# A linear-attention block and an MLP mixer in one kernel: y and the state products get PSUM banks of their own, and the masks change places

## The chip, the cores and the metric

The kernel runs on one core of one Trainium2 chip. A core has a matrix engine (TensorE, PE in the profile), three engines for elementwise work (VectorE, DVE; ScalarE, ACT; GpSimd, POOL) and a queue that issues transfers (SyncE, SP). Matrix products land in PSUM, which has eight banks of 512 fp32 values per partition; DVE and ACT take them out of it. The metric is the device time of one execution in microseconds (us). The kernel before takes 544.54 us, the median of three runs (543.99 to 545.38).

## The reference

The input is four sequences of 768 tokens with 8 heads of 48 channels. The first block is a recurrence with a state of 48 x 48 per head, the second an MLP mixer that takes its output as `x`, 384 channels per token. All is fp32.

```python
for t in range(S):
    cur = einsum('bhd,bhe->bhde', u * k[t], v[t])
    y[t] = einsum('bhd,bhde->bhe', r[t], state + cur)
    state = w[t][:, None] * state + einsum('bhd,bhe->bhde', k[t], v[t])
# mixer, on x = y with the heads side by side
xt = x.transpose(0, 2, 1)
u = x + (relu(xt @ w_tok1) @ w_tok2).transpose(0, 2, 1)
out = u + relu(u @ w_ch1) @ w_ch2
```

## The kernel before, in words

**Units.** The recurrence is cut into chunks of 64 tokens. A unit is 256 tokens of one sequence (two blocks of 128, four chunks) with all heads, so a sequence is three units and the whole is twelve (`NU`). Units 0 to 2 belong to the first sequence. For a unit, DVE scans the decays (`ends`, `begins`), multiplies keys and queries by them (`keys`, `queries`), PE makes the products of keys and queries inside each chunk (`gram`, line 248), and DVE writes them to `at` with a mask that keeps the strictly earlier tokens (`mask`, line 406). The token's own product, with `u`, goes to the diagonal of `at`: in units 0 to 3 by a second set of products (`own_gram`) that is picked out of PSUM with a predicated copy (`own_put`, line 260); in units 4 to 11 by sums that DVE makes from rows of r, k and `u_rows` (`products`, `sums_put`, lines 383 to 393).

**State.** `tokens` turns the keys with PE (line 278) and ACT copies them out (`copied`, line 279). `carry` (`outer`, line 295) makes the state products `kv`, one bank for each parity of chunk. Then four pairs follow each other: ACT scales the state (`scaled`, line 419), DVE adds `kv` to it (`updates`, lines 427 and 429).

**Output.** `across` (line 308) multiplies the scaled states by the queries into `y` in PSUM. A tiny ACT copy from `y` (`seen`, line 314) stands behind it. `within` (line 322) adds `at` times v to the same `y`, and ACT copies `y` to `x` in three pieces (`taken`, line 328).

**PSUM.** The pool `ps_a` has one tile of two banks under the tag "a", which both `kv` and `y` use; unit 2 alone takes its `kv` from `ps_m`. While units 0 to 2 are issued, `ps_g` holds two grams of two banks and `ps_m` two single banks. After that both are closed and `ps_m` has six single banks for all else: grams, turned keys, and the mixer's results. A tile's bank goes to the next tile once the last instruction that reads the first has ended.

**Mixer.** It works a sequence behind: `hidden` and `back` (lines 497 to 506) mix tokens, `turn` (line 512) transposes, `up` (line 520, with a relu on ACT at line 522) and `quarters` or `down` (lines 591 to 652) mix channels, and a result `o` is stored per 128 tokens. The last sequence uses another form of `up` (`thirds`, line 552).

**Weights.** They come as 64-bit floats in two raw buffers, `scratch` and `spare`, and are converted by DVE and ACT in steps (`convert`, lines 200 to 218; ACT's are lines 203, the power, and 209, the sign). A raw buffer is loaded again once its last reader has ended (line 197).

**Order.** PE, DVE and ACT issue in exactly the order in which `strict` receives the steps (line 88); SP's transfers are placed by the compiler's scheduler. For units 0 to 2 that order is a list written out by hand (lines 700 to 708). For units 3 to 11 each unit has a list of steps with costs (line 676), and `woven` (line 46) merges the lists of three units with the pieces of the mixer by the midpoints of their costs, as shares of each list's total. The range test (`ranges`, line 348) is an ACT step in these lists. The function `by_halves` is a path for inputs outside the range and is not run here.

## Time and profile before

| | |
|---|---|
| median of three runs | 544.54 us |
| the profiled execution, its own time | 542.25 us |
| its span | 540.5 us |
| PE busy, share of the span | 503.2 us, 93% |
| DVE busy | 335.9 us, 62% |
| ACT busy | 212.4 us, 39% |
| mean granted clock of TensorE | 0.981 |
| PE busy from 0 to 57 us (units 0 to 2) | 34.2 us |
| DVE busy from 0 to 57 us | 46.3 us |
| PE busy from 57 to 135 us (units 3 and 4 begin) | 72.8 us |
| PE busy from 290 to 390 us | 99.7 us |

The span is that of one profiled execution, from its first to its last instruction; the execution's own time is 1.75 us more, and the median of the runs without a profile another 2.29 us more. In rows of the timeline the numbers are the start and the length in us, then the engine, the line of the program, the operation, what it writes from what it reads, the shape and how many are merged into the row; in brackets stands how long the engine had been idle before, and what ended that. In rows of the waits the numbers are the total in us, how often, and the longest. One fp32 product stands as two matmul records. In rows of the windows they are start and end, length, PE's busy time and records, the granted clock as a share of full speed, the busy share of the transfer engines and GB/s.

### The profile page before, as it was taken

What the parts mean: (1) busy time and instruction counts of PE and PEld (TensorE: products, weight loads), DVE (VectorE), ACT (ScalarE), POOL (GpSimd) and SP (SyncE); (2) the same over time, 40 slices, a digit from 0 to 9 for tenths busy, and PEclk for the clock granted to TensorE, in tenths of its full rate; (3) what the DMA queues carried; (4) which work ended last, traced back from release to release, by engine and by line L of the source; (5) the groups of instructions that cost most, each with busy time, mean ns of one, the idle gap of its engine ahead of it and who ended that gap; (6) DMA issues with size and microseconds to landing.
All of it is one profiled execution on the core that took longest, in us unless ns stands there. A gap on an engine that the chain in (4) does not pass through costs nothing.

```text
span 540.5 us, 12631 instructions
## 1 busy us (share of the span) xinstructions
PE 503.2 (93%) x5542; PEld 434.2 (80%) x5542; DVE 335.9 (62%) x514; ACT 212.4 (39%) x525; POOL 1.3 (0%) x10
## 2 busy tenths in 40 slices
PE   3468889899799999999899999999999999999997
PEld 3356568677698967898898967898898977999996
DVE  7987899878671755194372656277295525775654
ACT  3857686571134333423324233523514313541400
POOL 0000000000000000000000000000000000000000
PEclk9689999899899999999999999999999999999999
DMA  8867647723212404104113112102000000000000
GB/s 312 330 178 190 232 156 237 185 78 104 84 59 70 119 29 129 46 16 150 37 59 107 52 59 98 31 3 89 2 24 7 2 31 1 1 1 31 1 32 32
DMA packets 20941, 46.01 MB, mean 85 GB/s; under 512 B 2128, under 2 KB 13008, under 8 KB 20880
## 3 DMA queue, kind: packets, MB, share of 16 engines
q1 hardware_dynamic: 20736, 45.14, 26.4%
q8 instruction: 45, 0.74, 0.6%
q14 instruction: 16, 0.13, 0.1%
q10 hardware_dynamic: 144, 0.00, 0.0%
HBM read 40.41 MB, written 4.72 MB: 83 GB/s over the span
## 4 chain that ended last, share of the span: by engine, by line
PE 83%; DVE 11%; ACT 4%; issue 1%; DMA 1%; DVEq 0%; ACTq 0%
PE q_ps L609 27%; PE z_ps L520 24%; PE z_ps L552 6%; PE h_ps L497 5%; PE h_ps L504 5%; PE gram L248 3%; PE h_ps L591 3%; PE y_ps L308 3%; PE y_ps L322 2%; PE kv_ps L295 2%; PE k_ps L278 2%; DVE to_end L356 1%; PE xT_ps L512 1%; DVE w L364 1%; ACT before L419 1%
## 5 line engine op out<-in xcount | busy, mean ns | idle before, releaser
L520 PE MATMUL z_ps<-xT,wch 128*128 128x256 f32 x648 | 148.6, 384 | 1.1 <-DVE wch L218 1.0
L520 PEld LDWEIGHTS z_ps<-xT,wch 128*128 128x128 f32 x648 | 121.1, 191 | 18.2 <-DVE wch L218 1.4
L609 PE MATMUL q_ps<-wch,z 128*128 128x192 f32 x492 | 87.0, 328 | 0.0
L609 PEld LDWEIGHTS q_ps<-wch,z 128*128 128x128 f32 x492 | 80.4, 190 | 1.3 <-DVE z L651 0.3
L522 ACT ACTIVATE z<-z_ps 128x256 f32<-128x256 f32 x108 | 40.9, 382 | 83.0 <-PE z_ps L520 82.2
L609 PE MATMUL q_ps<-scratch,z 128*128 128x192 f32 x324 | 58.1, 333 | 0.0
L419 ACT ACTIVATE before<-state,to_end 112x48 f32<-112x48 f32 x176 | 44.2, 324 | 27.0 <-DVE state L429 25.7
L609 PEld LDWEIGHTS q_ps<-scratch,z 128*128 128x128 f32 x324 | 54.4, 194 | 0.2
L429 DVE TENSOR_TENSOR state<-before,kv_ps 112x192 f32<-112x192 f32 x40 | 13.9, 349 | 42.8 <-ACT before L419 29.7
L504 PE MATMUL h_ps<-h,wtok 128*128 128x384 f32 x96 | 35.4, 493 | 0.6 <-ACT h L499 0.6
L497 PE MATMUL h_ps<-x,wtok 128*128 128x384 f32 x96 | 32.2, 489 | 1.3 <-DVE state L429 1.3
L619 DVE TENSOR_TENSOR o<-x,z 128x192 f32<-128x192 f32 x8 | 2.9, 358 | 47.6 <-ACT z L618 46.7
L506 DVE TENSOR_TENSOR x<-x,h_ps 128x384 f32<-128x384 f32 x24 | 13.3, 552 | 28.2 <-PE h_ps L504 28.1
L356 DVE TENSOR_TENSOR_SCAN to_end<-w,starts 112x1041 f32<-112x1041 f32 (+1 forms) x13 | 28.1, 2160 | 2.1 <-DMA w<-in_w_dram 1.7
L497 PEld LDWEIGHTS h_ps<-x,wtok 128*128 128x128 f32 x96 | 17.9, 190 | 13.2 <-issue 1.6
L364 DVE TENSOR_TENSOR_SCAN w<-w,starts 112x1041 f32<-112x1041 f32 x12 | 27.8, 2320 | 0.0
L348 ACT ACTIVATE junk<-to_end,least 112x1041 uint8<-112x1041 f32 x12 | 13.9, 1161 | 28.3 <-DVE to_end L356 28.3
L328 ACT COPY x<-y_ps 64x384 f32<-64x384 f32 (+1 forms) x36 | 17.1, 474 | 19.6 <-PE y_ps L322 19.3
L308 PE MATMUL y_ps<-before,rk 48*64 48x48 f32 x704 | 14.5, 226 | 11.0 <-DVE state L429 10.9
L504 PEld LDWEIGHTS h_ps<-h,wtok 128*128 128x128 f32 x96 | 16.6, 190 | 10.1 <-ACT h L499 2.8
L308 PEld LDWEIGHTS y_ps<-before,rk 48*64 48x64 f32 x704 | 13.1, 140 | 14.3 <-issue 9.4
L513 ACT COPY xT<-xT_ps 128x384 f32<-128x384 f32 x24 | 11.3, 476 | 22.5 <-PE xT_ps L512 22.4
(136 smaller groups left out, 665.8 us busy)
## 6 DMA issues: line engine op xcount, KB each, us to landing
rk<-in_rk_dram SPq DMA_DIRECT2D x36, 192.0 KB, 3.7
near<-in_near_dram SPq DMA_DIRECT2D x8, 768.0 KB, 4.4
w<-in_w_dram SPq DMA_DIRECT2D x11, 520.5 KB, 3.4
spare<-in_w_ch_dram SPq DMA_DIRECT2D x10, 512.0 KB, 4.5
vt<-in_v_dram SPq DMA_DIRECT2D x12, 384.0 KB, 4.6
out_dram<-o SPq DMA_DIRECT2D x24, 192.0 KB, 1.9
scratch<-in_w_ch_dram SPq DMA_DIRECT2D x8, 512.0 KB, 4.7
rk<-in_rk_dram SPq DMA_DIRECT2D x6, 512.0 KB, 8.5
```

The source lines that it names most:

```text
L248: fours(lambda q, j, rows, cols: pe.matmul(g[q][cols, ts(ca, T)], k_[rows, ds(ca * 128 + j * T, T)], r_[rows, ds(ca * 128 + j * T, T)], st ...
L308: pe.matmul(y[put(q, j), q, ds((c * A + a) * D, D)], r_[q * P:q * P + D, ds((c * A + a) * 128 + j * T, T)], before[g][q * P:q * P + D, a, ...
L328: return [lambda: act.copy(x[:, 0], got[:, 0])] + [lambda n=n: act.copy(x[ts(n, P), 1], got[ts(1 - n, P), 1]) for n in range(2)]
L356: dve.tensor_tensor_scan(to, of, start, 0.0, op0=ALU.mult, op1=ALU.add)
L364: dve.tensor_tensor_scan(w_[:ROWS], w_[:ROWS], starts[:ROWS], 0.0, op0=ALU.mult, op1=ALU.add)
L419: act.mul(t[:ROWS, a], state[bt, g][:ROWS, a], by_last(c, j)[:, a:a + 1])
L497: pe.matmul(sums[i], wtok1[:, c, ts(i, 128)], x_of()[:, c, :], start=(c == 0), stop=(c == C - 1))
L504: pe.matmul(ps, wtok2[:, i, ts(c, 128)], h1[:, i, :], start=(i == 0), stop=(i == DTOK // 128 - 1))
L520: pe.matmul(ps, wch1[:, m, ts(jt, 128)], xT[:, m, ts(s, SEG)], start=(m == 0), stop=(m == DM // 128 - 1))
L522: act.activation(zs[s][:, jt, :], ps, AF.Relu)
L552: pe.matmul(ps[:, q], lefts[r][:, ts(q, 128)], of[r], start=first and q == 0, stop=end and q == JB - 1, skip_group_check=True)
L609: pe.matmul(ps, a[:, j, :], b[:, j, :], start=(j == 0), stop=(j == HJ - 1))
```

## The change

It has four parts.

1. *Banks.* `kv` of all units of the first sequence (0 to 2) is put in the two single banks of `ps_m`; from unit 3 on it stays in `ps_a`. `y` of units 0 and 1 stays in `ps_a`, that of unit 2 goes to a tile of `ps_g`, and from unit 3 on `y` is two single banks of `ps_m`.
2. *Masks.* In units 0 to 3 the diagonal is put first, by a multiplication that writes all of `at` (with an fp32 mask that lies in `u_rows` until that is loaded), and the masked gram second, by a predicated copy. For unit 3 the diagonal's step moves from behind the mask to just behind its products, and the load of `u_rows` from the end of the hand-written list to behind that step.
3. *View.* The tiny copy from `y` is a step of its own, with a place in the lists; with `y` in two tiles it is two copies.
4. *Order.* The hand-written list of units 0 to 2 is rearranged.

```diff
--- before.py
+++ after.py
@@ -123,7 +123,8 @@
     ones = const.tile([128, 1], f32, name="ones")
     ident = const.tile([128, 128], f32, name="ident")
     strictly = const.tile([128, T], f32, name="strictly")
-    diagonal = const.tile([128, T], u8, name="diagonal")
+    on_diagonal = u_rows[:, :T]
+    diagonal, before_it = (const.tile([128, T], u8, name=name) for name in ("diagonal", "before_it"))
 
     def load_w(i):
         if i < NU:
@@ -166,11 +167,13 @@
 
     make_identity(nc, ident)
     for j in range(2):
-        dve.tensor_copy(diagonal[ts(j, T)], ident[ts(j, T), ts(j, T)])
+        dve.tensor_copy(on_diagonal[ts(j, T)], ident[ts(j, T), ts(j, T)])
+    dve.tensor_copy(diagonal, on_diagonal)
     pool.memset(strictly, 1.0)
     for j in range(2):
         pool.affine_select(out=strictly[ts(j, T)], in_=strictly[ts(j, T)], compare_op=ALU.is_gt, fill=0.0, base=0,
                            pattern=[[1, T]], channel_multiplier=-1)
+    dve.tensor_copy(before_it, strictly)
 
     wtok1 = wts.tile([128, C, DTOK], f32, name="wtok1")
     wtok2 = wts.tile([128, DTOK // 128, S], f32, name="wtok2")
@@ -296,36 +299,45 @@
                                   vt[ts(j, T), c, ts(2 * a + q, D)], start=True, stop=True)
         return kv
 
-    def across(r_, before, half):
-
-        y = ps_a.tile([128, 2, 512], f32, name="y_ps", tag="a")
+    def across(r_, before, half, where=None):
+
+        where = where or (ps_g and (ps_a, "a"))
+        both = where and where[0].tile([128, 2, 512], f32, name="y_ps", tag=where[1])
+        y = [both[:, q] for q in range(2)] if where else [bank("y_ps") for q in range(2)]
         begun = set()
         for c in range(UC):
             for a in range(A):
                 for q, j in ((0, 0), (1, 0), (1, 1), (0, 1)):
                     g = 2 * (half * UC + c) + j
                     if g > 0:
-                        pe.matmul(y[put(q, j), q, ds((c * A + a) * D, D)],
+                        pe.matmul(y[q][put(q, j), ds((c * A + a) * D, D)],
                                   r_[q * P:q * P + D, ds((c * A + a) * 128 + j * T, T)],
                                   before[g][q * P:q * P + D, a, :], start=(q, j) not in begun, stop=False,
                                   skip_group_check=True)
                         begun.add((q, j))
-        seen = apool.tile([128, 2], f32, name="seen")
-        act.copy(seen, y[:, :, X * D - 1])
-        return y
+
+        def see():
+            seen = apool.tile([128, 2], f32, name="seen")
+            if where:
+                act.copy(seen, both[:, :, X * D - 1])
+            else:
+                for q in range(2):
+                    act.copy(seen[:, q:q + 1], y[q][:, X * D - 1:X * D])
+
+        return y, see
 
     def within(y, at, vt):
 
         for ca in reversed(range(X)):
             c, a = divmod(ca, A)
             for q, j in ((0, 0), (0, 1), (1, 1), (1, 0)):
-                pe.matmul(y[put(q, j), q, ts(ca, D)], at[ts(j, T), q, ca, :], vt[ts(j, T), c, ts(2 * a + q, D)],
+                pe.matmul(y[q][put(q, j), ts(ca, D)], at[ts(j, T), q, ca, :], vt[ts(j, T), c, ts(2 * a + q, D)],
                           start=False, stop=ca == 0, skip_group_check=True)
 
     def put_in(x, y, half):
         x = x[:, ts(half, UC), :].rearrange("p c (a q e) -> p q c a e", a=A, q=2)
-        got = y[:, :, :X * D].rearrange("p q (c a e) -> p q c a e", c=UC, a=A)
-        return [lambda: act.copy(x[:, 0], got[:, 0])] + [lambda n=n: act.copy(x[ts(n, P), 1], got[ts(1 - n, P), 1]) for n in range(2)]
+        got = [y[q][:, :X * D].rearrange("p (c a e) -> p c a e", c=UC, a=A) for q in range(2)]
+        return [lambda: act.copy(x[:, 0], got[0])] + [lambda n=n: act.copy(x[ts(n, P), 1], got[1][ts(1 - n, P)]) for n in range(2)]
 
     def unit(i):
 
@@ -375,7 +387,8 @@
             L["own"] = grams(L.pop("uk"), r_)
 
         def own_put():
-            pick(at, diagonal, L.pop("own"))
+            for q, g in L.pop("own"):
+                dve.tensor_mul(at[:, q], g, over_heads(on_diagonal, g.shape[1]))
 
         def products(n):
             t = nears[i]
@@ -402,11 +415,13 @@
             L["gram"] = grams(k_, r_)
 
         def mask():
+            if i <= UB:
+                return pick(at, before_it, L.pop("gram"))
             for q, g in L.pop("gram"):
                 dve.tensor_mul(at[:, q], g, over_heads(strictly, g.shape[1]))
 
         def carry():
-            L["kv"] = outer(L.pop("kT"), vs[i], half, apart=i == UB - 1)
+            L["kv"] = outer(L.pop("kT"), vs[i], half, apart=bt == 0)
 
         def by_last(c, j):
             return of_chunks(L["to_end"], 1, 1)[:, :, 0].rearrange("p (x j) -> p x j", j=2)[:, ts(c, A), j]
@@ -431,7 +446,10 @@
         def before():
             if half == 0:
                 xs[bt] = xpool.tile([128, C, DM], f32, name="x")
-            L["y"] = across(r_, L["before"], half)
+            L["y"], L["see"] = across(r_, L["before"], half, (ps_g, "gram") if i == UB - 1 else None)
+
+        def seen():
+            L["see"]()
 
         def after():
             within(L["y"], at, vs[i])
@@ -446,7 +464,7 @@
         return dict(ranges=each(ranges, 2), ends=ends, keys=keys, begins=begins, queries=queries, own_u=each(own_u, A),
                     own_gram=own_gram, copied=each(copied, UC), taken=each(taken, 3),
                     own_put=own_put, products=[lambda n=n: products(n) for n in range(3)], sums_put=sums_put,
-                    tokens=tokens, gram=gram, mask=mask, carry=carry, before=before, after=after,
+                    tokens=tokens, gram=gram, mask=mask, carry=carry, before=before, seen=seen, after=after,
                     scaled=[lambda c=c, j=j: scaled(c, j) for c in range(UC) for j in range(2)],
                     updates=[lambda c=c, j=j: update(c, j) for c in range(UC) for j in range(2)])
 
@@ -675,12 +693,12 @@
         some = lambda fs, c: [(c, f) for f in fs]
         return [(0.1, lambda: (load_rk(i + 2), load_v(i + 1))), *([] if by_tokens else some(e["own_u"], 0.2)),
                 (2.4, e["ends"]), (1.2, e["keys"]), (0.4, e["ranges"][0]), (2.2, e["begins"]), (1.0, e["tokens"]), (0.2, e["copied"][0]),
-                *([] if by_tokens else [(1.0, e["own_gram"])]), (0.2, e["copied"][1]), (1.2, e["queries"]), (0.3, by[0]),
+                *([] if by_tokens else [(1.0, e["own_gram"]), (1.3, e["own_put"]), (0.1, lambda: sp.dma_start(u_rows, u_all))]), (0.2, e["copied"][1]), (1.2, e["queries"]), (0.3, by[0]),
                 (1.0, sums[0]), (1.0, e["carry"]), (1.0, sums[1]),
                 (0.7, up[0]), (0.3, by[1]), (1.4, e["gram"]), (1.0, sums[2]), (0.1, lambda: load_near(i + 1)),
                 (0.7, up[1]), (0.3, by[2]), (1.2, e["mask"]), (0.7, up[2]), (0.3, by[3]),
-                (1.3, e["sums_put"] if by_tokens else e["own_put"]), (0.4, e["ranges"][1]), (0.7, up[3]),
-                (0.1, lambda: load_w(i + 2)), (1.0, e["before"]), (1.0, e["after"]), *some(e["taken"], 0.3),
+                *([(1.3, e["sums_put"])] if by_tokens else []), (0.4, e["ranges"][1]), (0.7, up[3]),
+                (0.1, lambda: load_w(i + 2)), (1.0, e["before"]), (0.1, e["seen"]), (1.0, e["after"]), *some(e["taken"], 0.3),
                 *(some(make_lefts(i - NU + UB), 0.7) if i >= NU - UB else [])]
 
     hiddens, turned, ups, downs = mixing_of(0)
@@ -698,14 +716,14 @@
     s0, s1, s2 = (e["updates"] for e in (e0, e1, e2))
     t0, t1, t2 = (e["scaled"] for e in (e0, e1, e2))
     strict(*e0["own_u"], e0["ends"], e0["own_gram"], e0["begins"], e0["keys"], e0["tokens"], *e0["copied"], e0["queries"], lambda: load_w(2),
-           e0["gram"], *e1["own_u"], e1["ends"], e0["carry"], *e0["ranges"], e0["mask"], e0["own_put"], e1["own_gram"], s0[0], t0[1],
-           x0, p0, s0[1], t0[2], m0, g0, e1["begins"], s0[2], t0[3], add0, s0[3], t1[0], e0["before"], put0, load2,
+           e0["gram"], *e1["own_u"], e1["ends"], e0["carry"], *e0["ranges"], e0["own_put"], e0["mask"], e1["own_gram"], s0[0], t0[1],
+           x0, p0, s0[1], t0[2], m0, g0, e1["begins"], s0[2], t0[3], add0, s0[3], t1[0], e0["before"], e0["seen"], put0, load2,
            e1["keys"], e0["after"], *e2["own_u"], e1["tokens"], *e1["copied"], e1["queries"], e1["carry"], *e0["taken"], lambda: load_v(2),
-           e1["gram"], e2["ends"], e2["keys"], s1[0], t1[1], e2["tokens"], e2["begins"], e2["copied"][0], s1[1], t1[2], e2["copied"][1],
-           e2["carry"], e1["mask"], s1[2], t1[3], e1["own_put"], e2["own_gram"], s1[3], t2[0], e2["queries"], e2["gram"], e1["before"],
-           s2[0], t2[1], x1, p1, m1, e1["after"], s2[1], t2[2], e2["mask"], *h[:4], s2[2], t2[3], e2["own_put"], *e1["taken"], add1, g1,
-           s2[3], e2["before"], put1, to_ch[0][0], e2["after"], *h[4:8], x2, m2, *e2["taken"], p2, add2, g2, *h[8:], put2,
-           lambda: (load_w(3), load_rk(3), load_v(UB), load_w(4), load_rk(4)), to_ch[1][0], lambda: sp.dma_start(u_rows, u_all))
+           e1["gram"], e2["ends"], e2["keys"], s1[0], t1[1], e2["tokens"], e1["own_put"], e2["own_gram"], s1[1], t1[2], *e2["copied"],
+           e2["begins"], e2["carry"], s1[2], t1[3], e1["mask"], s1[3], t2[0], e1["before"], e2["queries"], e2["gram"], s2[0], t2[1], e1["seen"],
+           e1["after"], x1, m1, s2[1], t2[2], e1["taken"][0], *h[:4], e2["own_put"], s2[2], t2[3], e1["taken"][1], p1, e2["mask"], e1["taken"][2],
+           s2[3], e2["before"], e2["seen"], add1, g1, put1, to_ch[0][0], e2["after"], *h[4:8], x2, m2, *e2["taken"], p2, add2, g2, *h[8:], put2,
+           lambda: (load_w(3), load_rk(3), load_v(UB), load_w(4), load_rk(4)), to_ch[1][0])
 
     six_banks.close()
     ps_g, ps_m = None, six_banks.enter_context(tc.tile_pool(name="ps_m", bufs=6, space=bass.MemoryType.PSUM))
@@ -825,7 +843,8 @@
                         else:
                             dve.tensor_mul(new[:ROWS], states[g][:ROWS], by[:, ts(c, A), j].unsqueeze(2).to_broadcast([ROWS, A, D]))
                             dve.tensor_add(new[:ROWS], new[:ROWS], got)
-            y = across(r_, states, half)
+            y, see = across(r_, states, half)
+            see()
             within(y, at, vt)
             for f in put_in(x, y, half):
                 f()
```

## The prediction

> **What bounds the kernel now.** First the page: TensorE (PE) is busy for 503.2 of 540.5 us and carries 83% of the chain that ended last, so a microsecond counts only where PE idles or runs slowly. Its whole idle time is 37 us. The waits of PE name most of it (total us, times, longest):
>
> ```profile
> PE y_ps L308 <- DVE state L429: 10.9, 4, 3.9
> PE gram L248 <- DMA rk<-in_rk_dram: 8.3, 1, 8.3
> PE kv_ps L295 <- ACT x L328: 2.0, 1, 2.0
> ...
> PE y_ps L322 <- ACT seen L314: 1.1, 4, 0.3
> ```
>
> The first row is the change's subject: line 308 (`across`) waits for a state update. The PE timeline finds the four places (start, duration; idle before in brackets):
>
> ```profile
> 23.15 1.94 PE L308 MATMUL y_ps<-before,rk 48*64 48x48 f32 x48 [3.86 <-DVE state L429]
> ...
> 102.51 1.14 PE L308 MATMUL y_ps<-before,rk 48*64 48x48 f32 x48 [2.01 <-DVE state L429]
> 103.58 2.55 PE L520 MATMUL z_ps<-xT,wch 128*128 128x256 f32 x6
> 106.06 1.74 PE L322 MATMUL y_ps<-vt,at 64*64 64x48 f32 x64
> ...
> 143.44 1.15 PE L308 MATMUL y_ps<-before,rk 48*64 48x48 f32 x64 [3.54 <-DVE state L429]
> 144.51 3.80 PE L609 MATMUL q_ps<-scratch,z 128*128 128x192 f32 x12
> ...
> 265.91 1.15 PE L308 MATMUL y_ps<-before,rk 48*64 48x48 f32 x64 [1.50 <-DVE state L429]
> ```
>
> They are units 0, 3, 4 and 7. What PE lacked at 143 us is seen on VectorE (DVE) and ScalarE (ACT):
>
> ```profile
> 137.78 0.35 DVE L429 TENSOR_TENSOR state<-before,kv_ps 112x192 f32<-112x192 f32 x1
> ...
> 140.44 1.28 DVE L393 COPY_PREDICATED at<-diagonal,sums 128x1024 f32<-128x1024 uint8 x1
> ...
> 142.95 0.34 DVE L429 TENSOR_TENSOR state<-before,kv_ps 112x192 f32<-112x192 f32 x1
> ...
> 138.16 1.01 ACT L419 ACTIVATE before<-state,to_end 112x48 f32<-112x48 f32 x4 [2.84 <-DVE state L429]
> ```
>
> Line 308 reads the states scaled on ACT, complete at 139.2. It started at 143.44, 0.15 after the last update at 142.95, whose result only the next unit uses. That update reads `kv` from the two banks that `y` is about to take: the wait is for the banks. At unit 3 likewise: scaled at 99.7, last update at 102.11.
>
> The idle costs more than itself. At 144.51 twelve records take 3.80 us; the same group takes 2.11 elsewhere. The granted clock (start:end, length, PE busy, clock) says why:
>
> ```profile
> 141.00:142.00 1.00, 0.00 (x0) 1.00 0.00 0
> 145.00:146.00 1.00, 1.00 (x5) 0.50 0.47 94
> ```
>
> **What the Trainium skill says.** "TensorE: Matmul & The Clock Gate", Part 1: after an idle window of about 3.4 us the clock falls to half until a busy window has passed. The trace agrees: 0.50 after idles of 2.01 and 3.54, full speed after 1.50. "PSUM — Partial Sum Buffer", bank collisions: two engines may not touch one bank in one quadrant together; so `y`, `kv` and the view of `y` must wait for each other. The rows above agree. The same page (Engine vs sequencer instructions) calls ACT's and DVE's queues strict first-in, first-out: this prices the moved view. "VectorE: DVE Perf Modes", Why PSUM operands drop a tier: fp32 from PSUM gets the 1x mode; line 406 (multiply) 1199 ns and line 260 (predicated copy) 1304 ns agree.
>
> **Banks of y and kv, units 3 to 11** (`kv` in ps_a, `y` in two of the six ps_m banks). I laid the old and new step lists against the mixer pieces by their cost midpoints, as line 46 does; the old order so found agrees with the trace.
>
> Unit 4. PE ends its piece at 139.9 with the scaled states there since 139.2. `across` runs 139.9 to 141.0; the next product needs line 651's first sum (done 138.9) and ends 143.0 at full clock; `within` (line 322) needs the diagonal (141.7) and runs to 144.1. It ended at 149.4: gain 3.54 idle + 1.7 half clock = **5.3**.
>
> Unit 7. PE ready at 264.4, states scaled at 261.9: gain **1.5**; no slow clock followed.
>
> Unit 3 is harder. PE is free at 100.5, the states at 99.7. Here the diagonal's DVE operation moves from 99.8 to about 85, ahead of three updates: up to 1.3 later for them, less waits of 0.4 and 0.6 that DVE has on that stretch. So `across` starts about 100.7 instead of 102.5. But the view of `y` now follows one mixer piece later on ACT, behind all this:
>
> ```profile
> 100.12 1.16 ACT L348 ACTIVATE junk<-to_end,most 112x1041 uint8<-112x1041 f32 x1
> ...
> 101.26 1.14 ACT L203 ACTIVATE scratch<-scratch,rebias 128x1024 uint16<-128x1024 uint16 x1
> 102.30 0.37 ACT L522 ACTIVATE z<-z_ps 128x256 f32<-128x256 f32 x1
> 102.57 1.13 ACT L209 ACTIVATE scratch<-spare 128x1024 bf16<-128x1024 int32 x1
> 103.70 0.16 ACT L314 COPY seen<-y_ps 128x2 f32<-128x2 f32 x1
> ```
>
> With ACT some 1.3 late, a relu more (0.3) and two views (0.35), they end at 105.4; PE, done with `across` and its piece at 102.9, waits 2.5 before `within`, which ends 106.6 against 107.7. Gain 1.1 at full clock; half clock again would take up to 1.7. So the bounds are a gain of 1.8 (ACT not late at all) and a loss of 0.6; I take **0.5**, with the opening's loss below in it.
>
> **View as a step.** `y` in two tiles: two ACT copies of 0.16, hidden except where `within` follows. By the new order a relu piece stands between `across` and the view in units 3, 6 and 9: relu 0.35 + two views 0.32 + hand-overs about 0.08 = 0.75, where now the piece covers everything. Units 6 and 9: **loss 1.5**. In unit 10 view and `within` are adjacent, 0.28 now, 0.44 then: **loss 0.2**. Elsewhere the piece between is emptied by DVE or comes after the view: nothing; without that cover 0.35 each.
>
> **Opening, units 0 to 2** (`kv` in the two ps_m banks, `y` in ps_a, for unit 2 in ps_g). Added: two small DVE copies at 0.19, on DVE's chain near 10 us: +0.3. Diagonal first: one 1.2 multiply and one 1.3 predicated copy exchange places, sum equal. Unit 0: `across` needs only the scaled states (22.6), not the update (23.0): 0.5 gained, 0.2 left. Unit 1: `carry` (31.14) no longer waits for `y`'s copies: 29.5, gain 1.6; the first update moves from 32.4 to 31.3. Then the banks strike: unit 2's transposed keys need ps_m banks that `kv` of unit 1 holds until its third update. DVE from 31.3: update 0.25, diagonal 1.2, update 0.25, begins scan 2.25, third update, to 35.5. PE, empty since 32.3, waits 3.2: the cost of the new sharing, and a half-clock window. Only one bank is free by then, so transposes (0.95 at half clock), copy 0.6, transposes 0.95, copy 0.6 go in series to 38.6; scaling 0.9, fourth update at 39.7 (now 40.6). PE then does carry, `across`, gram, `within`, 4.5 in all, to 44.2 (now 43.95). The first hidden products end at 48.1 (now 48.3), unit 2's `within` at 50.6 (now 51.0): PE gains 0.3.
>
> Behind those transposes PE's queue holds unit 2's own gram, its `carry` and unit 1's `across`; the queries multiply on DVE overwrites what the own gram reads, and the scaling for unit 1's last update stands on ACT behind the second copy. So all three engines pass through this hole. Bounds: at full clock throughout, 0.9 less; at half clock until unit 2's `within`, about 2 more (line 308 took 1.94 instead of 1.10 in the half-clock stretch at 23 us, line 278 1.9 instead of 1.05). I take the window as worked out, because own gram and `carry` fill the one after it.
>
> One thing is late: the signs of the second weight pair come after unit 2's view, ending 50.6 instead of 49.55. They free `spare`, for which SP's load waits:
>
> ```profile
> 49.57 1.72 SPq L197 DMA_DIRECT2D spare<-in_w_ch_dram  x2
> ...
> 57.06 0.69 DVE L200 TENSOR_SCALAR scratch<-spare 128x1024 uint16<-128x1024 uint16 x1 [0.16 <-DMA spare<-in_w_ch_dram]
> ```
>
> The load lands 1.0 later; DVE's later wait of 0.84 for PE absorbs part on DVE, not on ACT: 0.7 stays on the conversions until PE's wait for `wch` at 70.2. This is in unit 3's 0.5.
>
> The `u_rows` load now waits for unit 3's diagonal, about 87. SP's loads behind it: the next w (86.71) 0 to 1 us late, which no scan reads before 108. Its reader is at 126.65: nothing. If SP held the weights behind it, up to 4 us.
>
> **Sum.** -5.3 - 1.5 - 0.5 + 1.5 + 0.2 = -5.6. On the profiled execution (542.25, span 540.5) that is 536.7 and 534.9; the median 544.54 stands 2.3 above it: **539.0**.
>
> **Rivals.** *(a) The opening gains too.* If the transposes of unit 2 are not held up, `carry`'s 1.6 and 1.8 of the opening's small PE waits (1.3 line 367, 1.3 line 497) come on top: -9.0, 535.5. Against: DVE is busy 46 of the first 57 us. *(b) The gain is eaten.* Half clock persists through unit 2 (+2) and returns at unit 3 (+1.7): -1.9, 542.6. For: the idle of 2.5 at unit 3 exceeds the 2.0 that sufficed before. *(c) Slower, by the banks of ps_m.* `y` needs two banks; if those last used by mixer pieces are chosen, `across` waits in each of nine units for ACT to empty them, behind scaling (1.0) and range test (1.35): up to 2.4 each. The trace of before shows no such wait, so the bounds are 0 and 2.4, and I take 0. To pass +0.3% it must eat 5.6 + 1.6 = 7.2, 0.8 per unit; at 1.0 the time is 547.9. Against: four banks stay for the mixer, whose ACT rows of 0.38 empty one piece in well under the 1.3 that PE takes to make it; gram and keys have given their banks back before `across`. *(d) The edit does not free line 308*, because the scaled states were what it lacked: excluded by 139.2 against 143.44.
>
> **How the numbers follow.** Likeliest 0.58 (own range 536.5 to 541.5), (a) 0.12, (b) 0.15, (c) and like losses 0.15. No change means within 0.3% (1.6 us), about what a measurement of this kernel tells apart. (b) straddles it: half faster, half same. So faster 0.77, same 0.08, slower 0.15. Range 534.5 to 544.5: it leaves out (c) and the far end of (a).
>
> **What would show it.** Right: line 308 without waits on line 429 after 60 us; full clock at 140 to 150; new waits of 0.7 before `within` in units 6 and 9 on the view, of about 2.5 in unit 3; a PE hole before the third unit's transposes. Wrong: line 308 waiting for ACT or for evacuations, more than 1 us later arrival at 70, half clock past 107.

## The result and the profile after

The changed kernel takes 544.07 us (median of 22 runs, 542.75 to 546.10), the kernel before 544.89 in 22 runs beside it (542.23 to 546.94): ratio 0.9991, 95% interval 0.9976 to 1.0005. That is no change. 539.0 was predicted, within the range of 534.5 to 544.5 only by 0.4 us and with a chance of 0.08 for "within 0.3%". Of the rivals, (b), "the gain is eaten", comes nearest.

The profiled execution of the changed kernel took 546.10 us, its span is 544.3, its mean clock 0.971. The pair of traces differs by 3.8 us and the medians by -0.8: the execution that was profiled before had a clock of 0.981, while 27 others of the same kernel, in the last set of runs, stood at 0.959 to 0.978 and took 543.4 to 547.9 us, so one execution's share of half clock has to be kept apart from the change. Places in the two traces are therefore compared below, and sizes are taken from medians.

The waits of PE after (total us, times, longest):

```profile
PE k_ps L281 <- issue: 4.4, 1, 4.4
PE y_ps L334 <- ACT seen L325: 3.3, 4, 1.9
...
PE y_ps L313 <- ACT before L434: 2.3, 2, 1.2
PE q_ps L627 <- DVE z L668: 2.2, 1, 2.2
```

The row "y_ps L308 <- DVE state L429: 10.9" is gone, so part 1 of the change does what it says (line 313 is `across` now). Four rows have come. Where they lie, the PE timeline shows (start, duration; idle before in brackets):

```profile
35.56 1.08 PE L281 MATMUL k_ps<-ident,rk 128*128 128x128 f32 x4 [4.42 <-issue]
...
104.63 0.99 PE L313 MATMUL y_ps<-before,rk 48*64 48x48 f32 x28 [1.08 <-ACT before L434]
...
109.06 1.31 PE L334 MATMUL y_ps<-vt,at 64*64 64x48 f32 x64 [1.95 <-ACT seen L325]
...
144.29 3.86 PE L627 MATMUL q_ps<-scratch,z 128*128 128x192 f32 x12 [2.19 <-DVE z L668]
148.07 1.15 PE L313 MATMUL y_ps<-before,rk 48*64 48x48 f32 x64
...
230.14 1.20 PE L334 MATMUL y_ps<-vt,at 64*64 64x48 f32 x64 [0.52 <-ACT seen L325]
```

In order: the hole before unit 2's transposes; unit 3's `across`, which has its banks but lacks the last scaled state; unit 3's `within` behind the view; a product in front of unit 4's `across`; unit 6's `within` behind the view. Unit 4's `across` itself no longer waits, and yet unit 4 has gained nothing: PE now stands idle for 2.19 one group of products earlier, and the twelve records behind that take 3.86 instead of 2.11.

The windows of PE in the opening (start and end, length, busy time, clock, transfers):

```profile
40.00:42.00 2.00, 2.00 (x67) 0.50 0.04 8
...
48.00:50.00 2.00, 2.00 (x6) 0.83 0.63 185
```

In finer windows the clock falls at 35.0 and comes back at 48.7, 13.7 us later. Between 38.4 and 48 PE is busy without a break and still at half clock; in the trace of before it stands at 1.00 from 36 on. Behind unit 3's `within` it falls again, from 110.1 to 113.5 (before from 104.0 to 107.4), and with the wait on line 668 from 144.2 to 147.7.

Against the trace of before, the end of `within` stands 2.6 later in unit 3, 3.0 in unit 4, 3.6 in unit 6, 2.1 in unit 7 (whose 1.5 was gained) and 2.7 from unit 10 on; the last store lands 1.1 later after DVE's end. Of the 2.6, the first 2.4 are there at 53 us, at the end of the opening.

What unit 4's missing microseconds are is seen on DVE:

```profile
136.73 0.94 DVE L401 TENSOR_REDUCE sums<-near 128x16 f32<-128x768 f32 x1
137.60 0.54 DVE L613 TENSOR_TENSOR o<-x,h_ps 128x384 f32<-128x384 f32 x1
...
142.89 0.36 DVE L637 TENSOR_TENSOR o<-x,z 128x192 f32<-128x192 f32 x1 [4.48 <-DMA out_dram<-o]
143.28 0.96 DVE L668 TENSOR_TENSOR z<-z 128x768 f32<-128x768 f32 x1
```

and on SP's queue:

```profile
137.71 0.35 SPq L151 DMA_DIRECT2D near<-in_near_dram  x1
138.17 0.36 SPq L614 DMA_DIRECT2D out_dram<-o  x1
```

Before, DVE made the second half of the result `o` first (132.59) and the sums of unit 4 after it (133.05), and SP issued both stores at 131.43 and 133.16 and the load of the next rows (`near`, 768 KB) at 134.02:

```profile
131.43 2.09 SPq L596 DMA_DIRECT2D out_dram<-o  x2
134.02 0.34 SPq L150 DMA_DIRECT2D near<-in_near_dram  x1
```

Now the sums stand ahead of that half. They are the last reader of `near`, so the load is free at 137.7 and goes out ahead of the store of 192 KB. The store lands 4.6 us after its issue (1.9 before). There is one `o` buffer: line 637, which fills it again, waits 4.48 for the landing, line 668 stands behind it, and PE needs line 668. The new order comes from the step lists: the diagonal has moved inside unit 3's list and the view, priced at 0.1, has joined each, so the midpoints of `woven` have moved and two steps have exchanged places. Which of the two did it is seen in the run with the early diagonal below.

The theory to be tested: the banks are worth what was predicted or more, and three other parts of the change give it back, which are the order in unit 4, the opening, and the view with the early diagonal of unit 3. The rivals: the bank sharing was not worth 7 us in the first place; or the new banks of `y` cost on their own, by crowding `ps_m`.

### The profile page after: what moved, and what is told of

The parts are those of the page before. It is cut to its first block, busy times and chain, and to the rows that moved or that the text cites. A ratio compares the mean times of both kernels' runs of the same rounds, so it can differ in the third digit from the quotient of the medians.

```text
span 544.3 us, 12657 instructions
## 1 busy us (share of the span) xinstructions
PE 509.1 (94%) x5542; PEld 439.9 (81%) x5542; DVE 336.0 (62%) x516; ACT 212.6 (39%) x534; POOL 1.3 (0%) x10
## 4 chain that ended last, share of the span: by engine, by line
PE 79%; DVE 11%; ACT 4%; issue 3%; DMA 1%; DVEq 0%; ACTq 0%
PE q_ps L627 27%; PE z_ps L538 22%; PE z_ps L570 6%; PE h_ps L515 5%; PE h_ps L522 4%; PE h_ps L609 3%; PE y_ps L334 3%; PE gram L251 2%; PE kv_ps L298 2%; PE y_ps L313 2%; PE k_ps L281 2%; DVE to_end L368 1%; ACT scratch L212 1%; PE xT_ps L530 1%; DVE scratch L218 1%
## 5 line engine op out<-in xcount | busy, mean ns | idle before, releaser
L434 ACT ACTIVATE before<-state,to_end 112x48 f32<-112x48 f32 x176 | 44.2, 323 | 34.4 <-DVE state L444 31.7
L281 PE MATMUL k_ps<-ident,rk 128*128 128x128 f32 x96 | 15.4, 311 | 6.2 <-issue 4.4
L334 PEld LDWEIGHTS y_ps<-vt,at 64*64 64x64 f32 x768 | 14.5, 148 | 7.3 <-ACT seen L325 4.6
L334 PE MATMUL y_ps<-vt,at 64*64 64x48 f32 x768 | 16.0, 234 | 4.6 <-ACT seen L325 3.3
```

Of the source, the lines that this page charges most:

```text
L281: pe.transpose(both[c][:, a, :], k_[:, ts(c * A + a, 128)], ident)
L334: pe.matmul(y[q][put(q, j), ts(ca, D)], at[ts(j, T), q, ca, :], vt[ts(j, T), c, ts(2 * a + q, D)], start=False, stop=ca == 0, skip_group_c ...
L434: act.mul(t[:ROWS, a], state[bt, g][:ROWS, a], by_last(c, j)[:, a:a + 1])
```

## The experiments

**Unit 4's sums behind the store.** In the changed kernel, unit 4's last step of the sums is taken at the place of the load, behind the last piece of `down`.

```diff
-(1.4, e["gram"]), (1.0, sums[2]), (0.1, lambda: load_near(i + 1)),
+(1.4, e["gram"]), (1.0, (lambda: None) if i == UB + 1 else sums[2]),
+(0.1, lambda: ((sums[2]() if i == UB + 1 else None), load_near(i + 1))),
```

> The changed kernel with one exchange: DVE's sums of unit 4 stand after the last result of the first 256 tokens is added, not before it, so that result's store is issued ahead of the 768 KB load of the next rows. Theory 'store': the changed kernel's hole of 2.19 us in unit 4 and the half clock after it (1.75) come from that store landing 4.6 us after its issue instead of 1.9; expected: no wait on line 668, the second matmuls of y in unit 4 end 4.3 us earlier relative to unit 3, time 544.1 - 4.3 = 539.8. Rival 'chance': the landing varies from 2 to 5 us whatever is ahead of it; then the wait stays or comes and goes, and the time is 544.

541.50 us, ratio 0.9927 (0.9896 to 0.9957). SP's queue and PE in that kernel:

```profile
135.91 2.10 SPq L614 DMA_DIRECT2D out_dram<-o  x2
138.51 0.34 SPq L151 DMA_DIRECT2D near<-in_near_dram  x1
```

```profile
142.27 2.11 PE L627 MATMUL q_ps<-scratch,z 128*128 128x192 f32 x12
144.31 1.15 PE L313 MATMUL y_ps<-before,rk 48*64 48x48 f32 x64
```

The stores go first, line 637 waits 0.92 instead of 4.48, PE has no wait, and the twelve records take 2.11. From the end of unit 3's `within` to that of unit 4's it is 37.3 us, against 42.1 in the changed kernel and 41.6 before. One exchange of two steps is shown to cost 0.64%: 3.5 us in medians, where 4.3 was expected, and 3.9 between the profiled executions. The wait and the slow records are 2.19 + 1.75 = 3.9; the 4.8 from unit 3 on is more because unit 3 itself lost 0.75 in this trace, at half clock from 106.3 to 113.1.

**The banks of y alone.** The kernel before, with nothing but `y` of units 3 to 11 in two single banks; the view stays where it was, as two copies.

```diff
-        y = ps_a.tile([128, 2, 512], f32, name="y_ps", tag="a")
+        both = ps_g and ps_a.tile([128, 2, 512], f32, name="y_ps", tag="a")
+        y = [both[:, q] for q in range(2)] if ps_g else [bank("y_ps") for q in range(2)]
...
-        act.copy(seen, y[:, :, X * D - 1])
+        if ps_g:
+            act.copy(seen, both[:, :, X * D - 1])
+        else:
+            for q in range(2):
+                act.copy(seen[:, q:q + 1], y[q][:, X * D - 1:X * D])
```

> The kernel before, with one part of the change alone: y of units 3 to 11 in two of the six single banks, its view (two copies) where it stood; opening, masks and order as before. Theory 'the freed banks are worth it': waits of y on the state update vanish in units 3, 4 and 7 with the half clock behind two of them: -2.8, -5.2 and -1.5 us, so 544.9 - 9.5 = 535.4. Rival 'the six banks are too few': across waits for ACT or DVE to empty its two banks, 1 us or more in each of nine units, and the time is 544.9 or above.

534.16 us, ratio 0.9819 (0.9784 to 0.9854). Repeated later on another chip:

> The kernel before with y's banks alone once more, beside the kernel with the diagonal first: 534.2 expected from the first time.

535.19 us, ratio 0.9802 (0.9773 to 0.9831). PE in the first:

```profile
138.87 1.15 PE L309 MATMUL y_ps<-before,rk 48*64 48x48 f32 x64
139.95 2.22 PE L614 MATMUL q_ps<-scratch,z 128*128 128x192 f32 x12
142.09 1.15 PE L327 MATMUL y_ps<-vt,at 64*64 64x48 f32 x64
```

No idle and no slow record: from unit 3's `within` to unit 4's it is 36.4 us, 5.2 less than before. Of the waits of line 308, only unit 0's 3.9 is left. This is the fastest version of the study, ahead of both kernels. Both rivals of the theory fall: the shared banks were worth some 10 us in medians, and `across` meets no wait for a bank in units 3 to 11. Between the two profiled executions it is 7.7: units 3, 4 and 7 gain 2.8, 5.2 and 1.6, and 1.8 is lost by the end of unit 2, where the two programs are alike.

**The old opening.** The changed kernel with the banks, masks and list of units 0 to 2 as before (the view keeps its place behind `across` there).

```diff
-            L["kv"] = outer(L.pop("kT"), vs[i], half, apart=bt == 0)
+            L["kv"] = outer(L.pop("kT"), vs[i], half, apart=i == UB - 1)
...
-            L["y"], L["see"] = across(r_, L["before"], half, (ps_g, "gram") if i == UB - 1 else None)
+            L["y"], L["see"] = across(r_, L["before"], half)
```

> The changed kernel with units 0 to 2 as in the kernel before (list, banks, order of the two masks, view), from unit 3 on as changed. Theory 'opening': the hole of 4.4 us before the third unit's transposes, and the half clock from 35 to 48 us after it, cost 2.4 us at the first 16 hidden products after unit 2, and all of it reaches the end: 541.7. Rival 'covered': the weight conversions on DVE and ACT bind up to 70 us whatever PE does before, and the time is 544.

542.26 us, ratio 0.9953 (0.9936 to 0.9970): 0.38% better than the changed kernel, 2.1 us. The waits on line 668 (2.2) and of unit 3's `within` (1.9) stay, as they should. So the new opening is a loss of about 2, where a gain of 0.3 was forecast. That is a loss in medians, not in every execution. From the end of unit 0 to that of unit 2 the old opening takes 23.7 to 24.7 us in four traces of this study, and 28.0 to 28.2 in three others, in which half clock lasts to 51 us and longer (three parts undone, the early diagonal, and the banks alone the second time). The new opening takes 26.4 to 27.0 in four traces: two of the changed kernel, the first experiment and the next one.

**The view at once.** The changed kernel with the view of units 3 to 11 right behind `across`.

```diff
+            if i >= UB:
+                L["see"]()
 
         def seen():
-            L["see"]()
+            if i < UB:
+                L["see"]()
```

> The changed kernel with the view of y in units 3 to 11 right behind the products with the states, as before the change; all else as changed. Theory 'view': the waits of the second matmuls of y on the view, 1.95 us in unit 3 and 0.52 in units 6 and 9, shrink to below 0.3; the time falls by 2 to 3 to 541.5. Rival: in unit 3 the view is late because ACT is late, not because of the relu ahead of it; then about 1.5 of the 1.95 stays and the time is 543.

542.38 us, ratio 0.9953 (0.9936 to 0.9970), again 2.1 us better. Units 6 and 9 lose their waits of 0.52 each and end 0.64 earlier each. Unit 3 waits 0.80 instead of 1.95, but that is not the view:

```profile
105.12 2.44 PE L541 MATMUL z_ps<-xT,wch 128*128 128x256 f32 x6
108.36 2.06 PE L334 MATMUL y_ps<-vt,at 64*64 64x48 f32 x64 [0.80 <-ACT seen L325]
```

The six records ahead of `within` take 2.44 instead of 1.56, since PE is at half clock from 105.6 to 112.5 here, and that hides 0.9 of the wait; `within` ends at 110.42, where the changed kernel ended it at 110.37. In the run with three parts undone, which has the view at the same place and full clock there, the wait is 1.68. So the rival holds for unit 3: the view is late because ACT is late. In the traces units 6 and 9 give 1.3 of the gain and unit 3's view some 0.3; the rest is not traced to a place, because the clock differs between the two.

**The hole filled.** Two kernels add products of 128 x 128 that nothing reads to the opening's hole, so that PE isn't idle: 32 of them and 14. They are to tell whether the hole costs by its length or by the clock.

```diff
+    def keep_busy():
+        t = ps_a.tile([128, 2, 512], f32, name="idle_ps", tag="a")
+        for n in range(14):
+            pe.matmul(t[:, n % 2, :128], ident, ident, start=True, stop=True)
...
-           e1["gram"], e2["ends"], e2["keys"],
+           e1["gram"], keep_busy, e2["ends"], e2["keys"],
```

> The changed kernel with 32 products of 128 x 128 added, whose results nothing reads, into a bank pair that is free then: they stand between unit 1's gram and unit 2's transposes, where PE is empty for 4.4 us. The transposes still wait for the banks. Theory 'idle sets the clock': with the hole filled, the granted clock stays at 1.0 from 35 to 48 us, where it was 0.5, and the hidden products after unit 2's y start some 2 us earlier; time 544.1 - 2 = 542. Rival 'small products': the products of 48 and 64 rows that fill 38 to 47 us don't hold the clock whatever went before; it falls to 0.5 by 42 us and the time is 544.

547.97 us, ratio 1.0045 (1.0023 to 1.0066); two of its 16 runs took 554.99 and 671.77, the second at a mean clock of 0.75; they are left out of the ratio and stay unexplained. The 32 products took 7.41 us and held the transposes up to 39.83, so this run was mis-sized: it says that the clock was 1.00 from 33 to 49, but not what that is worth.

> The changed kernel with 14 products of 128 x 128 in PE's empty stretch before unit 2's transposes instead of the 32 of the run before, which took 7.4 us where 4.4 were empty and so delayed the transposes by 4.3. At 0.227 each, 14 take 3.2 us and end before the banks come free. Their results are not read. Theory 'idle sets the clock': transposes where the changed kernel has them (35.6), granted clock 1.0 from 36 to 47, first hidden products at about 45.5 instead of 47.45, time 544.1 - 2 = 542. Rival 'small products': half clock by 42 all the same, first hidden products at 47, time 544.

543.58 us, ratio 0.9968 (0.9952 to 0.9985), with 14 products. PE there:

```profile
32.72 3.51 PE L721 MATMUL idle_ps<-ident 128*128 128x128 f32 x28
36.07 0.60 PE L281 MATMUL k_ps<-ident,rk 128*128 128x128 f32 x4
...
44.33 2.97 PE L515 MATMUL h_ps<-x,wtok 128*128 128x384 f32 x8
```

The transposes start 0.5 later than in the changed kernel, but take 0.60 instead of 1.08, the clock is 1.00 from 33 to 70, and the hidden products start at 44.33 instead of 47.45. Some of that is lost again in a new idle of 1.39 at 51.2. In medians 0.2% is left, about 1.3 us, of the 2 that the theory expected, and its interval overlaps that of the changed kernel. So the trace shows that the clock alone holds the hidden products back by 3.1 us; that most of the opening's loss is the clock and not the hole is likely, and not shown.

**Three parts undone together.** The edits of the first, third and fourth experiment in one kernel; what is left of the change is the banks of `y` and unit 3's early diagonal.

> The changed kernel with the three edits of the earlier runs together: sums of unit 4 after the store, opening as before, view at once. What is left of the change is y of units 3 to 11 in banks of its own, and in unit 3 the diagonal ahead of the updates and of the mask. Theory 'the parts add': -3.5, -2.1 and -2.1 from 544.1 give 536.4, some 2 us above the kernel with nothing but the banks of y (534.2), because unit 3's updates come 1.3 us later on DVE and y waits for the scaled states. Rival 'the diagonal's place costs nothing': 534.2.

538.14 us, ratio 0.9855 (0.9819 to 0.9890). In shares of the kernel before that is 1.36% less than the changed kernel, where the three alone give 0.64 + 0.38 + 0.38 = 1.40%: they add. But it doesn't reach the banks alone, which points at the early diagonal.

**The early diagonal of unit 3.** The kernel with the banks of `y` alone, and unit 3's diagonal put first, with the masked gram picked and `u_rows` loaded behind it.

```diff
-                *([] if by_tokens else [(1.0, e["own_gram"])]), (0.2, e["copied"][1]), ...
+                *([] if by_tokens else [(1.0, e["own_gram"]), (1.3, e["own_put"]),
+                                        (0.1, lambda: sp.dma_start(u_rows, u_all))]), (0.2, e["copied"][1]), ...
-                (1.3, e["sums_put"] if by_tokens else e["own_put"]), (0.4, e["ranges"][1]), ...
+                *([(1.3, e["sums_put"])] if by_tokens else []), (0.4, e["ranges"][1]), ...
```

> The kernel before with the banks of y and one part of the change more: in unit 3 the diagonal first, at its new early place, the masked gram picked in after it, and the load of u_rows behind it. Theory 'late updates': DVE's updates of unit 3 move back by 1.3, y waits for the scaled states by about 1.1 and its second matmuls for the view by some 0.5 more; 2.0 above the kernel with the banks alone: 536.2. Rival 'places are equal': the same time as the banks alone.

538.75 us, ratio 0.9859 (0.9831 to 0.9888), against 0.9802 (0.9773 to 0.9831) for the banks alone beside it. PE with the early diagonal:

```profile
106.38 0.99 PE L312 MATMUL y_ps<-before,rk 48*64 48x48 f32 x28 [1.07 <-ACT before L432]
...
110.55 1.25 PE L330 MATMUL y_ps<-vt,at 64*64 64x48 f32 x64 [1.68 <-ACT seen L322]
```

and without it:

```profile
105.14 1.14 PE L309 MATMUL y_ps<-before,rk 48*64 48x48 f32 x48
...
108.49 1.25 PE L327 MATMUL y_ps<-vt,at 64*64 64x48 f32 x64 [0.73 <-ACT seen L319]
```

1.07 inside `across` and 0.95 more ahead of `within`: 2.0 us, in the two places where the changed kernel waits 1.08 and 1.95. On DVE the third update stands at 105.61 with it and at 103.01 without, though PE runs 0.15 earlier with it up to unit 2's `within`. The medians differ by 3.6; both kernels have two groups of times (see the end), and group against group it is 1.7 (535.72 to 534.03) and 1.4 (538.84 to 537.47).

This run also tells what exchanged the two steps of unit 4. Its lists from unit 3 on are those of the changed kernel but for the view's step, and SP issues as before the change:

```profile
135.43 2.09 SPq L609 DMA_DIRECT2D out_dram<-o  x2
138.02 0.34 SPq L151 DMA_DIRECT2D near<-in_near_dram  x1
```

Both stores go ahead of the load, and DVE waits 0.92 for the landing. So it took the view's step, priced at 0.1 in lists that add up to some 24, to put the load ahead of the store.

**Unit 0's y in a gram tile.** On top of the banks alone, `y` of unit 0 goes to `ps_g`, so that it doesn't wait 3.9 for the banks of its `kv`.

```diff
+both = ps_g and (ps_g.tile([128, 2, 512], f32, name="y_ps", tag="gram") if early else ps_a.tile(...))
-            L["y"] = across(r_, L["before"], half)
+            L["y"] = across(r_, L["before"], half, i == 0)
```

> The kernel with nothing but the banks of y, and unit 0's y in a gram tile as well, so that unit 1's carry need not wait for y's copies. Theory 'carry': it starts 1.3 us earlier, DVE's first update of unit 1 moves from 32.4 to 31.3, and 1 us reaches the end: 533.2. Rival 'DVE binds the opening': the 1.3 us are lost in front of DVE's begins scan and the mask; 534.2.

535.17 us, ratio 0.9814 (0.9787 to 0.9842): nothing over the banks alone. The wait of 3.9 was the longest of the four, and of these the only one whose removal gained nothing. In the traces unit 0 ends 1.8 earlier than with the banks alone (26.29 against 28.11) and unit 2 at the same time (52.85 and 52.82), with half clock from 35.0 to 48.6 in between; whether DVE or the clock takes the gain back is not shown.

**Both kernels once more**, one profiled execution each, for what in the traces is chance.

> The kernel before once more, for a second trace. The first was of a fast execution (542.25 against a median of 545). All theories expect the waits of y on the state update in units 0, 3, 4 and 7 again; where the 2 to 3 us of a typical execution go is open: the landing of the first loads (8.3 us then) or half clock in the opening.

> The changed kernel once more, for a second trace. All theories expect the hole before unit 2's transposes, half clock after it, the view's wait in unit 3 and line 668's wait in unit 4 again; if one of them is missing, it was chance in the first trace.

Before: 541.60 us, line 308 waiting 10.2 in four places; the changed kernel: 545.93, the hole of 4.42, half clock from 35 to 48.6 and again after unit 3's `within`, 1.95 at unit 3's view and 2.22 on line 668. All four losses are there again, so they belong to the kernel. The two pairs also agree on the sign: both profiled executions of before lie below the medians of their kernel, by 2.6 and 3.1, and both of the changed kernel above its median, by 2.0 and 1.9. So the traces differ by some 4 us twice, where the medians differ by -0.8; no run shows why. One thing of before was not there again: the half clock behind unit 3's `across`; `within` took 1.15 and not 1.74.

## Why the prediction was wrong

For the banks themselves it was right in units 4 and 7: 5.3 and 1.5, where the banks alone gained 5.2 and 1.6. Unit 3's 0.5 was the net of banks, diagonal and view; the banks alone gained 2.8 there (1.2 against the second trace of before, which has no half clock there). That 5.3 + 1.5 + 0.5 = 7.3 is close to the 7.7 between the profiled executions is chance. Four losses stand against the banks' gain: unit 4's order, the opening, the early diagonal of unit 3 and the view.

- **"Unit 4 ... gain 5.3": right as a mechanism, and not to be had.** The banks alone show 5.2. The step that failed is the one that took DVE's chain as it stood ("the next product needs line 651's first sum (done 138.9)"). The new lists had been laid against the pieces, but the prediction names no exchange in unit 4, and does not ask which DMAs the exchanged steps release. The price was 3.5 us in medians, by the exchange of two transfers on a queue that the prediction had looked at for `u_rows` and the weights alone. No wait on the `u_rows` load is seen, as it said.
- **"Opening ... PE gains 0.3": 2.1 lost.** The hole was foreseen, at 3.2 (4.42 measured; the extra 1.2 is PE done at 31.1 and not 32.3), the transposes in series through one bank too, and the updates, forecast from 31.3 on, with the third done at 35.5 and the fourth at 39.7, began at 31.20 and were done at 35.46 and 40.40. What failed is "I take the window as worked out, because own gram and `carry` fill the one after it". They filled it and the next one, from 38.4 to 45.3, and the clock stayed at 0.50 for 13.7 us in all; what this says of the rule that the step rests on stands in the last section. Its own bound, "at half clock until unit 2's `within`, about 2 more", was the right end: 2 less the 0.3 is 1.7, against 2.4 in the trace and 2.1 in medians. The hole's length did no more harm, since it ends at 35.56 as forecast (35.5).
- **"Unit 3 ... I take 0.5": lost, by a term.** Of the view's wait, 2.5 was forecast and 1.95 came. The `across` forecast for 100.7 began at 102.87, which is the opening's 2.4 later than 100.5, but it stopped after 20 records for 1.08 until a state was scaled. What failed is the term "up to 1.3 later" for DVE's updates, less two waits of 1.0: with the early diagonal the third update came 2.6 later. The step counts what the diagonal adds to DVE but not that the new order also puts the first update behind three more steps of the weights: at 97.24 instead of 93.78 (early diagonal and banks alone). The early diagonal costs 2.0 alone in the traces.
- **"Units 6 and 9: loss 1.5": right as a mechanism, a little high.** The waits are 0.52 each, and `within` ends 0.6 later in each, 1.2 in all. Unit 10's "loss 0.2" did not come: 0.28 after as before.
- **"Unit 7: gain 1.5": right.** The offset to before falls from 3.6 to 2.1 there.
- **"The median ... stands 2.3 above it"**: this carried an offset of the kernel before over to the changed one, whose median stands 2.0 below its profiled execution. On profiled executions the forecast was 536.7 against 546.10, 9.4 off; that the forecast of the median is only 5.1 off, and 544.07 just inside the range, is luck.
- **Rivals.** (b), at 542.6, named half clock in the opening and at unit 3 as what eats the gain. Both are seen, the second from 110.1 to 113.5, one window late, after the view's 1.95 and not after 2.5; it is in only one of the two traces of before, and in both of the changed kernel. The largest loss, unit 4's, was in no rival. (c) is refuted by the banks alone, and (a) by the hole.

In medians, as shares of before: the banks alone -1.9% (mean of 0.9819 and 0.9802); the early diagonal of unit 3 +0.4% (from there to the three parts undone, 0.9855), the view +0.4%, the opening +0.4%, unit 4's order +0.6%: -0.1%, as measured. That the shares add is shown for three of them. The diagonal's is the remainder between two kernels, so the sum has to close; measured directly beside the banks alone it is 0.6%, and 1.4 to 1.7 us (0.3%) by groups.

## What to carry to other kernels

When a change shifts the midpoints of a planned order, list every pair of steps that exchanges places and ask of each which transfer it releases and what buffer that transfer guards; here a step priced at 0.1 exchanged one such pair, and that cost a third of the gain. Before an idle of PE is priced, ask what runs behind it: here small products behind a hole of 4.4 us left the clock at half for 13.7 us. Of a change with several parts, try the one that the profile asks for alone: the two banks for `y` by themselves were worth 10 us, the whole change nothing.

## What the runs showed of the hardware

- *The windows of the clock can be read off a trace.* "TensorE: Matmul & The Clock Gate", Part 1, gives a free-running window of 3.413 us. In the changed kernel the clock falls at 35.0, 110.1 and 144.2: 22.0 and 10.0 such windows apart, which agrees. The prediction's rule, that the clock falls after an idle window, is too strict: less idle sufficed, and the measurement decides. In the windows ahead of the last two falls PE was idle for 1.95 and 2.1 of the 3.4, ahead of the fall at 105.6 with the view at once for 1.1. And 1.9 did not suffice in the second trace of before (99.9 to 103.4), so idle time alone is not what counts.
- *A window that is busy by the profile does not always bring the full clock back.* The same section has the clock return after one busy window. In the changed kernel PE was busy with products of 48 and 64 rows through two whole windows, and the clock stayed at 0.50; it came back after the window up to 48.7, in which the first 128 x 384 products ran from 47.45:

```profile
38.43:41.84 3.41, 3.41 (x111) 0.50 0.03 5
41.84:45.25 3.41, 3.41 (x134) 0.50 0.67 216
```

With 32 filling products, though, a window with nothing but small products in it did bring the clock back, before the filling began at 32.58:

```profile
28.98 1.84 PE L298 MATMUL kv_ps<-vt,kT 64*64 64x48 f32 x59 [0.30 <-ACT kT L282]
...
30.65 2.00 PE L251 MATMUL gram<-rk 48*64 48x64 f32 x63
...
29.10:32.50 3.40, 3.40 (x126) 0.50 1.04 298
32.55:35.90 3.35, 3.35 (x33) 1.00 0.80 197
```

So did one in the second trace of before (31.7 to 35.1). Neither busy time nor the size of the products alone decides. An estimate from the records points at the amount of work: rows x columns x width, summed over a window, is some 21 million in each of the two windows that stayed at half clock and 24 million in each of the two that left it. Over the half-clock windows of all fourteen traces, those below 22.6 stayed and those above 23.8 left; in between both occur. No run varied this amount, so what counts was not settled.
- *One kernel, two times.* The banks alone ran in 533.7 to 534.5 or in 537.2 to 537.5 us, with one run between at 535.97, clock 0.98 or 0.97. In the trace of the shorter kind the half clock of the opening ends at 37.5, in the other at 51.5. A window that falls differently on the same idles would do that; no run here set its phase.
- *A store behind a load.* 192 KB landed 1.9 us after issue, and 4.6 when 768 KB had been issued on the same queue 0.46 us before. "DMA: Bandwidth & Descriptors", Queues, rings and completion order, says that each transfer engine takes up descriptors of a queue in the order of the ring; the load itself took 4.6, so the 2.7 us agree with waiting for the larger part of it.
